# Row sums transposed before their reciprocal, a priority for each step of an attention pair, and a first moment for each weight piece

## The chip, the cores and the metric

The kernel runs on one core of one Trainium2 chip. A time is the device time of one execution in microseconds; "before" is the median of three runs. The core has five queues of instructions that run in order: TensorE (PE, with its weight loads PEld), VectorE (DVE), ScalarE (ACT), GpSimd (POOL) and SyncE (SP), which issues all DMAs here.

## The reference

```python
# 4 batches x 8 heads, 576 positions, head_dim 64
scores = q @ k.T / sqrt(64)
scores = where(block_i >= block_j, scores, -1e9)      # causal by blocks of 64
attn = exp(scores - max(scores))
attn = attn / (sum(attn) + 1e-9)
x = (attn @ v) as 2304 tokens x 512
for w_in, w_out, c in ((moe..., 1.0), (moe2..., 1.702)):
    h = x @ w_in                                      # 512 -> 2048
    x = (h / (1 + exp(-c * h))) @ w_out               # 2048 -> 512
```

The inputs of attention are float32; the weights arrive in float64 and are converted on the chip. Products are made with a high and a low part of each operand (three matmuls in place of one).

## The kernel before

Attention works on 16 pairs (`NP`) of heads; a pair lies on 128 partitions, 64 for each head. For a pair the steps are: load q, k, v; split them into high and low parts (`q_hi`, `q_lo`, `k_hi`, `k_lo`, `v_hi`, `v_lo`) and lay q out as block diagonals (`q_put`, a DMA); for each of nine query blocks j the scores (`s_mm`), their maximum (`s_max`, L423, VectorE) and the exponential (`s_exp`, L433, ScalarE), which also leaves the row sums in column j of the tile `l`; transposes of the exponentials in seven groups (`t_mm`, L472, TensorE), evacuated as a high part (`t_hi`, ScalarE, one of them VectorE) and a remainder (`t_lo`, L490, VectorE); the output products (`o_mm`, L509) and their copies (`o_copy`); three shifts by DMA (`x_shift`), a sum (`x_add`, L537) and a normalization (`x_norm`, L542) on GpSimd.

The row sums go their own way. `r_inv` adds 1e-9 (L439) and takes the reciprocal (L440) of a 128 x 9 tile on VectorE; `r_mm` transposes it into PSUM (L444); `r_copy` copies the 9 x 128 result to SBUF on ScalarE (L450); `r_put` writes it to DRAM (L457) and `r_get` reads it back broadcast (L463), for `x_norm`.

The PSUM banks are handed out in order: scores have fixed banks by j, transposes take turns in banks 4 and 5 (`ring`, `take`), and the transpose of the row sums takes its turn there too, after groups 0, 2 and 6 and before 3, 4, 5 and 1. Output products take turns in banks 6 and 7.

The two feed-forward layers follow: the 16 f-slices of a layer are taken in three passes (`SIZES`), in each pass the tokens in chunks of 512, per chunk and slice 12 matmuls up (L648 to L650), the gate (L663 to L668) and 12 matmuls down (L675 to L677). The weights come in pieces, two for each slice: a DMA of 512 KB into one of two raw buffers (L231), a conversion by ScalarE (L238), four VectorE instructions (L247, L249, L259, L261) and GpSimd (L269), and a split into high and low (L274, L275). Converted pieces of the first slices are made while attention still runs.

The order of all this comes from a planner in the kernel (`Flow`). Each step is added with an engine, an assumed duration, the buffers that it reads and writes, and a priority `at`; `run` then goes through time and lets each engine take, of the steps that are ready at that moment, the one with the lowest `at`. That order becomes the order of instructions in each queue. The chip then runs each queue in that order, whatever the real durations are. Steps of attention always go ahead of those of the feed-forward (`BEFORE`).

Before, the priority of an attention step was its place in the list `plan` (L545): an offset in whole pairs and its index, times `TAU` = 12.6. A weight piece was not ready before `EARLY`: 150 us for piece 0 and 7 us more for each further one, up to piece 8. SBUF pools of attention (`a1`, `a2`, `a3`) are closed and reopened for the feed-forward (`l1`, `l2`, `l3`) when all attention steps listed up to then are done (`ends`, L603).

Of the kernel before, what the change touches and what calls it, by code (L numbers as in the profile page):

```python
# [129 lines left out]
def block_causal_attention_two_ffn(  # L130
# [25 lines left out]
    NS = 10  # L156
    N1, N2 = 2, 3
    NWF = 8
    EARLY = (150.0, 7.0)
    NWARM = 12  # L160
    TAU = 12.6
    LEAD = 8
    BEFORE = 1e4
# [122 lines left out]

    ends = {"a1": [], "a2": [], "a3": []}
    clock = [0.0]

    def op(eng, us, fn, reads=(), writes=(), lag=0.0, size=0, sb=False):  # L290
        x = add(eng, us, fn, reads, writes, clock[0] - BEFORE, lag=lag, size=size, name="att", sb=sb)
        for y in ends:
            ends[y].append(x)
        return x

    def bd(p, i):
# [18 lines left out]
        return T("a3", shape or [P, S], dt, f"{n}_{p % 2}")  # L315

    def pt(p, i):
        return T("a2" if p % 2 == 0 else "a3", [P, nat, P], F32R, f"pt{i}_{p % 2}")

    def copy(eng, o, i):  # L320
        if eng == "act":
# [112 lines left out]
            o, t, AF.Exp, bias=mx_(p, j), scale=1.0, accum_out=ls[:, j:j + 1]),  # L434
            kb + [("mx", p % 2, j)], [kpj(p, j), ("l", p % 2, j)])

    def r_inv(p):
        r, ls = a3(p, "r", [P, NB]), a3(p, "l", [P, NB])
        op("dve", 0.16, lambda: nc.vector.tensor_scalar_add(r, ls, 1e-9), [("l", p % 2, j) for j in range(NB)], [("r", p % 2)])  # L439
        op("dve", 0.2, lambda: nc.vector.reciprocal(out=r, in_=r), [("r", p % 2)], [("r", p % 2)])  # L440

    def r_mm(p):
        b = take("t", ("rp", p))
        op("pe", 0.11, lambda: nc.tensor.transpose(bank[b][:NB, :P], a3(p, "r"), ident), [("r", p % 2), "ident"], [("B", b)],  # L444
           lag=0.2)

    def r_copy(p):
        b = held["rp", p]
        rt = a3(0, "rt", [NB, P])
        op("act", 0.16, lambda: nc.scalar.copy(rt, bank[b][:NB, :P]), [("B", b)], [("rt", 0)])  # L450

    def rd_(p):
        return T("drp", [2, NB, BLK], F32, f"rd{p % 2}")
# [25 lines left out]
    def t_hi(p, g, eng):  # L479
        b = held["t", p, g]  # L480
        n = len(groups[g]) * P
        t = bank[b][:, :n]
        o = pt_view(p, 0, g)
        op(eng, US[eng](n), copy(eng, o, t), [("B", b)], [("pt", p % 2, g, 0)])

    def t_lo(p, g):
        b = held["t", p, g]
        n = len(groups[g]) * P
        hi, lo = (pt_view(p, i, g) for i in range(2))
        op("dve", dve(n), lambda: nc.vector.tensor_sub(lo, bank[b][:, :n], f32(hi)), [("B", b), ("pt", p % 2, g, 0)],  # L490
           [("pt", p % 2, g, 1)])

    def o_mm(p, h, half):
        j0, j1 = halves[half]
        n = (j1 - j0) * BLK
        b = take("o", ("o", p, h, half))
        o = bank[b]
        va = va_(p)
        seq = [(i, kt) for i in (0, 1) for kt in range(NKT) if 2 * kt < j1]
        fs = {fidx[kt, j] for _, kt in seq for j in range(max(j0, 2 * kt), j1)}  # L500
        gs = [g for g, x in enumerate(groups) if fs & set(x)]

        def mms():
            for a, (i, kt) in enumerate(seq):
                js = max(j0, 2 * kt)
                f = fidx[kt, js]
                w = va[:, 2 * kt + h, :, :].rearrange("p a b -> p (a b)")
                x = pt(p, i)[:, f:f + j1 - js, h * BLK:(h + 1) * BLK]
                nc.tensor.matmul(o[:, (js - j0) * BLK:n], w, x, start=(a == 0), stop=(a == len(seq) - 1))  # L509

        us = sum(mm((j1 - max(j0, 2 * kt)) * BLK) * 1.05 for i, kt in seq)
        op("pe", us, mms, [("pt", p % 2, g, i) for g in gs for i in range(2)] + [("va", p % 2, 0), ("va", p % 2, 1)], [("B", b)], lag=0.2)

    def e_(p, h):
        return a3(p, f"e{h}")
# [23 lines left out]
    def x_norm(p):  # L539
# [2 lines left out]
        op("pool", 1.45, lambda: nc.gpsimd.tensor_mul(xy[:, hp, b * S:(b + 1) * S], x, rb),  # L542
           [("x", p % 2, 0), ("x", p % 2, 1), ("rb", p % 2, 0), ("rb", p % 2, 1)], xkeys(hp, b * S, S))

    plan = [  # L545
        (0, s_mm, 3), (1, s_exp, 4), (0, s_max, 3), (2, o_mm, 0, 0), (1, t_mm, 2), (1, t_hi, 0, "act"),
        (3, x_shift, 1), (0, s_exp, 3), (3, x_shift, 2), (0, s_mm, 7), (1, t_hi, 2, "act"),
        (2, o_mm, 0, 1), (-1, q_hi, "act"), (2, o_copy, 0, 0, "dve"), (0, s_mm, 0), (1, r_inv),
        (1, t_lo, 0), (1, t_mm, 6), (0, s_max, 7), (0, s_mm, 8), (1, t_lo, 2), (1, r_mm),
        (0, s_exp, 7), (1, load, "v"), (1, t_hi, 6, "act"), (1, t_lo, 6), (0, s_max, 0), (3, x_add), (-1, load, "k"),  # L550
        (2, o_copy, 0, 1, "act"), (-1, q_lo), (-1, q_put, 0), (0, s_mm, 2), (1, v_hi, "pool"),
        (-1, k_hi, "pool"), (-1, q_put, 1), (0, s_exp, 0), (2, x_shift, 0), (1, t_mm, 3),
        (3, x_norm), (0, s_mm, 6), (2, o_mm, 1, 0), (0, s_max, 2), (1, r_copy),
        (0, s_max, 8), (1, t_hi, 3, "act"), (1, t_mm, 4), (0, s_exp, 2), (0, s_mm, 5), (0, s_max, 6),
        (-1, k_lo, "pool"), (0, s_exp, 8), (-2, load, "q"), (1, t_lo, 3), (2, o_mm, 1, 1),
        (1, t_hi, 4, "act"), (0, s_exp, 6), (0, s_max, 5), (1, t_lo, 4), (2, o_copy, 1, 0, "act"),
        (0, s_exp, 5), (0, s_mm, 1), (1, t_mm, 5), (1, v_lo, "pool"), (1, t_mm, 1), (1, r_put),
        (0, s_max, 1), (0, s_mm, 4), (1, t_hi, 5, "dve"), (2, o_copy, 1, 1, "act"),
        (1, t_lo, 5), (0, s_exp, 1), (1, t_hi, 1, "act"), (2, r_get), (0, s_max, 4), (0, t_mm, 0),
        (1, t_lo, 1),  # L560
    ]

    def attention():
        clock[0] = -1e3
        load(0, "q")
        load(0, "k")
        load(1, "q")
        load(1, "k")
        warm = a1(0, "ql")[:, :512]
        op("dve", 0.5, lambda: nc.vector.memset(f32(warm), 0.0), (), [ka1(0, "ql")])  # L570
        op("pe", 4.7, lambda: [nc.tensor.matmul(bank[7], warm[:, :P], warm, start=True, stop=True) for _ in range(NWARM)],
           [ka1(0, "ql")], [("B", 7)])
        op("pool", 0.6, lambda: make_identity(nc, ident), (), ["ident"])
        op("pool", 0.1, lambda: nc.gpsimd.memset(one, 1.0), (), ["one"])
        for i in range(2):
            for k in range(2):
                t = bd(i, k)
                op("pool", 0.6, lambda t=t: nc.gpsimd.memset(f32(t[A, :, B]), 0.0), (), [("bd", i, k, 0)])
                op("pool", 0.6, lambda t=t: nc.gpsimd.memset(f32(t[B, :, A]), 0.0), (), [("bd", i, k, 1)])
            for j in range(0, NB, 2):  # L580
                op("dve", 0.1, lambda i=i, j=j: nc.vector.memset(pj(i, j)[:, (j + 1) * BLK:], 0.0), (), [kpj(i, j)])
        k_hi(0, "act")
        q, kq = src(0, "q")
        q = q.rearrange("p (j n) -> p j n", n=BLK)
        for h, r in enumerate((A, B)):
            op("act", 0.69, lambda r=r: nc.scalar.mul(bd(0, 0)[r, :, r], q[r], BLK ** -0.5), [kq], [("bd", 0, 0, h)])
        k_lo(0, "pool")
        for h, r in enumerate((A, B)):
            op("dve", 0.9, lambda r=r: q_sub(bd(0, 1)[r, :, r], q[r], bd(0, 0)[r, :, r]), [kq, ("bd", 0, 0, h)],
               [("bd", 0, 1, h)])  # L590
        for p in range(NP + 3):
            for i, (off, fn, *args) in enumerate(plan + [(0, None)]):
                clock[0] = p * TAU + i * TAU / len(plan)
                if fn and 0 <= p - off < NP:
                    fn(p - off, *args)
            if p in (NP - 1, NP, NP + 2):
                k = {NP - 1: 1, NP: 2, NP + 2: 3}[p]

                def swap(k=k):
                    stacks[f"a{k}"].close()  # L600
                    pools[f"l{k}"] = open_pool(ctx, f"l{k}")

                opened[f"l{k}"] = add("none", 0.0, swap, after=list(ends[f"a{k}"]) + [opened[x] for x in opened])  # L603
                ends.pop(f"a{k}")

# [111 lines left out]
    def feed_forward(t):  # L719
        for l in range(2):  # L720
            f0 = 0
            for i, size in enumerate(SIZES[l]):
                fs = list(range(f0, f0 + size))
                f0 += size
                for z, f in enumerate(fs):
                    n = l * NF + f
                    at = -100 + n if n < N1 else t + z * 5.4 - LEAD
                    for h in range(2):
                        o = functools.partial(add, at=at, early=EARLY[0] + EARLY[1] * min(piece(n, h), NWF))
                        w_load(o, n, h)  # L730
                        for stage in (w_scale, w_bits, w_rest, w_sum):
                            stage(o, n, h)
                        w_split(n, h, at)
                t = phase(l, fs, i == 0, i == len(SIZES[l]) - 1, t)
# [50 lines left out]
```

## Time and profile before

| | |
|---|---|
| median of three runs | 1017.42 us (1016.72 to 1021.14) |
| profiled execution | 1021.33 us, its span 1019.5 us |
| mean granted clock of TensorE | 0.993 |
| busy: PE, DVE, ACT, POOL | 988.3, 703.7, 482.5, 326.1 us |
| moved by DMA | 112.67 MB |

A busy share is a mean over stages: attention fills the first 205 us or so, the feed-forward the rest. Line numbers (L439) are those of the kernel before. "Idle before" and "waited for" name what came last before an engine went on; a wait on an engine that isn't the bottleneck costs nothing.

### The profile page before, as it was taken

How to read it: one execution, taken by the hardware profiler on the slowest of the kernel's cores; microseconds unless marked ns; L12 is line 12 of the kernel's file. 1: busy time of each engine (PE TensorE's matmuls, PEld its weight loads, DVE VectorE, ACT ScalarE, POOL GpSimd, SP SyncE). 2: the span in 40 equal slices, each digit the busy share in tenths (PEclk: the TensorE clock that was granted, in tenths of full speed). 3: DMA queues.
4: the chain of work that ended last, by engine and by line, in shares of the span. 5: the costliest groups of instructions: out<-in, count | busy, mean ns of one | idle time of the engine just before them, and what ended most of it. 6: DMA issues, size and time to landing. Idle time of an engine off the chain costs nothing.

```text
span 1019.5 us, 14413 instructions
## 1 busy us (share of the span) xinstructions
PE 988.3 (97%) x5196; PEld 846.5 (83%) x5196; DVE 703.7 (69%) x1144; ACT 482.5 (47%) x1055; POOL 326.1 (32%) x238
## 2 busy tenths in 40 slices
PE   7899998889999999999999999999999999999998
PEld 6888888867888888888888888888898888988887
DVE  6888888999999886749873359863269443444433
ACT  6778778755555452335432245533255222333221
POOL 7566665684444432216320026320035000000000
PEclk9999999989999999999999999999999999999999
DMA  7677779532333344422331111321112222112222
GB/s 188 157 184 184 185 177 219 151 110 92 135 124 138 133 163 166 138 78 86 133 126 61 42 33 61 136 83 42 42 62 83 83 83 83 63 62 83 84 83 83
DMA packets 84616, 112.67 MB, mean 111 GB/s; under 512 B 41920, under 2 KB 46528, under 8 KB 84544
## 3 DMA queue, kind: packets, MB, share of 16 engines
q1 hardware_dynamic: 84544, 111.74, 35.9%
q8 instruction: 41, 0.67, 0.3%
q14 instruction: 31, 0.25, 0.1%
HBM read 72.12 MB, written 23.67 MB: 94 GB/s over the span
## 4 chain that ended last, share of the span: by engine, by line
PE 73%; DVE 15%; ACT 4%; DMA 3%; issue 3%; POOL 1%; SPq 0%; DVEq 0%; ACTq 0%; POOLq 0%
PE bank L648 11%; PE bank L650 11%; PE bank L649 11%; PE sb L675 6%; PE sb L677 6%; PE sb L676 6%; PE bank L677 6%; PE bank L675 6%; PE bank L676 6%; PE bank L509 2%; PE bank L472 2%; DVE wf L249 2%; DVE xc L629 2%; ACT p L433 2%; DVE pt L490 2%
## 5 line engine op out<-in xcount | busy, mean ns | idle before, releaser
L665 DVE SCALAR_TENSOR_TENSOR th<-th,bank 128x512 f32<-128x512 f32 (+1 forms) x160 | 100.4, 629 | 203.6 <-ACT th L663 203.3
L648 PE MATMUL bank<-xc,ws 128*128 128x512 f32 (+1 forms) x640 | 236.6, 370 | 0.0
L649 PE MATMUL bank<-xc,ws 128*128 128x512 f32 (+1 forms) x640 | 236.1, 369 | 0.0
L650 PE MATMUL bank<-xc,ws 128*128 128x512 f32 (+1 forms) x640 | 236.0, 369 | 0.0
L663 ACT ACTIVATE th<-bank 128x512 f32<-128x512 f32 (+1 forms) x160 | 88.9, 556 | 294.1 <-PE bank L650 289.2
L275 POOL TENSOR_TENSOR ws<-wf,ws 128x512 fp32r<-128x512 f32 x64 | 91.7, 1442 | 205.4 <-ACT ws L274 205.4
L269 POOL TENSOR_TENSOR wf<-wf,wt 128x512 f32<-128x512 f32 x64 | 93.9, 1467 | 194.6 <-DVE wt L261 177.5
L667 ACT CAST g<-th 128x512 fp32r<-128x512 f32 (+1 forms) x160 | 92.3, 578 | 115.1 <-DVE th L665 115.0
L668 DVE TENSOR_TENSOR g<-th,g 128x512 fp32r<-128x512 f32 (+1 forms) x160 | 110.9, 695 | 43.4 <-ACT g L667 42.1
L650 PEld LDWEIGHTS bank<-xc,ws 128*128 128x128 f32 x640 | 120.9, 189 | 20.6 <-DVE xc L629 0.5
L648 PEld LDWEIGHTS bank<-xc,ws 128*128 128x128 f32 x640 | 121.2, 189 | 20.3
L649 PEld LDWEIGHTS bank<-xc,ws 128*128 128x128 f32 x640 | 121.1, 189 | 20.0
L677 PE MATMUL sb<-g,ws 128*128 128x512 f32 (+1 forms) x320 | 118.4, 370 | 2.4 <-DVE g L668 2.3
L675 PE MATMUL sb<-g,ws 128*128 128x512 f32 (+1 forms) x320 | 118.5, 370 | 1.6 <-DVE yst L710 0.5
L676 PE MATMUL sb<-g,ws 128*128 128x512 f32 (+1 forms) x320 | 117.8, 368 | 0.0
L675 PE MATMUL bank<-g,ws 128*128 128x512 f32 (+1 forms) x320 | 117.7, 368 | 0.0
L676 PE MATMUL bank<-g,ws 128*128 128x512 f32 (+1 forms) x320 | 117.7, 368 | 0.0
L677 PE MATMUL bank<-g,ws 128*128 128x512 f32 (+1 forms) x320 | 117.7, 368 | 0.0
L629 DVE TENSOR_TENSOR xc<-xy,xc 128x512 fp32r<-128x512 f32 (+1 forms) x120 | 90.9, 777 | 14.0 <-PE bank L649 8.5
L490 DVE TENSOR_TENSOR pt<-bank,pt 128x512 fp32r<-128x512 f32 (+1 forms) x112 | 68.7, 620 | 15.2 <-ACT pt L322 15.1
L627 ACT CAST xc<-xy 128x512 fp32r<-128x512 f32 (+1 forms) x120 | 66.8, 575 | 25.1 <-PE bank L649 23.7
L472 PE MATMUL bank<-ident,p 128*128 128x128 f32 x400 | 63.9, 284 | 11.1 <-DVE pt L490 9.7
(76 smaller groups left out, 1623.7 us busy)
## 6 DMA issues: line engine op xcount, KB each, us to landing
raw<-w SPq DMA_DIRECT2D x64, 512.0 KB, 3.5
yd<-yst SPq DMA_DIRECT2D x64, 256.0 KB, 2.4
yst<-yd SPq DMA_DIRECT2D x64, 256.0 KB, 4.1
v<-vP SPq DMA_DIRECT2D x16, 320.0 KB
k<-kT SPq DMA_DIRECT2D x16, 288.0 KB, 3.8
rb<-rd SPq DMA_DIRECT2D x32, 144.0 KB, 3.7
x<-e SPq DMA_DIRECT2D x32, 144.0 KB, 3.1
q<-qT SPq DMA_DIRECT2D x15, 288.0 KB, 3.6
```

Source lines behind the costliest of these rows:

```text
L269: op("pool", 1.27, lambda: nc.gpsimd.tensor_add(wf_(k), wf_(k), wt_(k)), [kw, kt], [kw])
L275: add("pool", 1.28, lambda: nc.gpsimd.tensor_sub(slot(n, i)[:, 1, :], wf_(k), f32(slot(n, i)[:, 0, :])), [kw, kh], [kl], at, after=slot_af ...
L629: add("dve", dve(n) + 0.01, lambda view=view, s=s: nc.vector.tensor_sub(view(1), s, f32(view(0))), xkeys(kt, c0, n) + [Kh], [Kl], tx, afte ...
L648: nc.tensor.matmul(h, w[:, 0, c], view(0), start=kt == 0, stop=False)
L649: nc.tensor.matmul(h, w[:, 1, c], view(0), start=False, stop=False)
L650: nc.tensor.matmul(h, w[:, 0, c], view(1), start=False, stop=kt == ND - 1)
L665: add("dve", dve(n), lambda th=th, h=h: nc.vector.scalar_tensor_tensor(out=th(), in0=th(), scalar=1.0, in1=h, op0=ALU.add, op1=ALU.mult), ...
L667: add("act", act(n) + 0.05, lambda th=th, g=g: nc.scalar.copy(g(0), th()), [kth], [kgh], t, after=e2)
L668: add("dve", dve(n) + 0.01, lambda th=th, g=g: nc.vector.tensor_sub(g(1), th(), f32(g(0))), [kth, kgh], [kgl], t, after=e2, sb=True)
L675: nc.tensor.matmul(y, w[:, 0, c], g(0), start=st, stop=False)
L676: nc.tensor.matmul(y, w[:, 1, c], g(0), start=False, stop=False)
L677: nc.tensor.matmul(y, w[:, 0, c], g(1), start=False, stop=sp)
```

## The change

The row sums `l` are transposed as they are (`r_mm` reads `l`); `r_inv` then runs on the 9 x 128 block: VectorE adds 1e-9 from PSUM into `rt` and takes the reciprocal in place. `r_copy` is gone. Each step of a pair gets a number of its own, in pair lengths from the pair's start, and the pairs are listed one after the other; each weight piece gets its own first moment; a pool is closed when the steps that read or write its own tiles are done. `NPT` = 2 leaves `pt` as it was. The explicit early load of k for pair 1 is left to the plan.

```diff
-    EARLY = (150.0, 7.0)
+    EARLY = [146.9, 164.9, 159.8, 120.4, 105.5, 214.8, 0.0, 153.2, 224.6, 111.5, 211.0, 126.0]
+    NPT = 2
...
-        for y in ends:
-            ends[y].append(x)
+        for k in [*reads, *writes]:
+            home = {"q": "a1", "k": "a1", "qh": "a1", "ql": "a1", "kh": "a1", "kl": "a1", "bd": "a1", "pj": "a2"}.get(k[0], "a3")
+            if k[0] == "pt" and NPT == 2 and k[1] == 0:
+                home = "a2"
+            ends[home].append(x)
...
-    def r_inv(p):
-        r, ls = a3(p, "r", [P, NB]), a3(p, "l", [P, NB])
-        op("dve", 0.16, lambda: nc.vector.tensor_scalar_add(r, ls, 1e-9), [("l", p % 2, j) for j in range(NB)], [("r", p % 2)])
-        op("dve", 0.2, lambda: nc.vector.reciprocal(out=r, in_=r), [("r", p % 2)], [("r", p % 2)])
-
     def r_mm(p):
         b = take("t", ("rp", p))
-        op("pe", 0.11, lambda: nc.tensor.transpose(bank[b][:NB, :P], a3(p, "r"), ident), [("r", p % 2), "ident"], [("B", b)],
-           lag=0.2)
-
-    def r_copy(p):
+        op("pe", 0.11, lambda: nc.tensor.transpose(bank[b][:NB, :P], a3(p, "l"), ident),
+           [("l", p % 2, j) for j in range(NB)] + ["ident"], [("B", b)], lag=0.2)
+
+    def r_inv(p):
         b = held["rp", p]
         rt = a3(0, "rt", [NB, P])
-        op("act", 0.16, lambda: nc.scalar.copy(rt, bank[b][:NB, :P]), [("B", b)], [("rt", 0)])
+        op("dve", 0.2, lambda: nc.vector.tensor_scalar_add(rt, bank[b][:NB, :P], 1e-9), [("B", b)], [("rt", 0)])
+        op("dve", 0.2, lambda: nc.vector.reciprocal(out=rt, in_=rt), [("rt", 0)], [("rt", 0)])
...
     plan = [
-        (0, s_mm, 3), (1, s_exp, 4), (0, s_max, 3), (2, o_mm, 0, 0), (1, t_mm, 2), (1, t_hi, 0, "act"),
...
+        (-2.723, load, "q"), (1.183, q_hi, "act"), (-1.280, load, "k"), (-0.183, q_lo), (-0.345, q_put, 0),
...
+        (4.531, s_exp, 3), (-0.564, s_mm, 7), (2.002, s_mm, 0), (-0.949, s_max, 7), (-0.149, s_mm, 8),
...
+        (1.031, s_exp, 8), (0.947, s_exp, 6), (0.482, s_max, 5), (-4.074, s_exp, 5), (3.642, s_mm, 1),
+        (-3.963, s_max, 1), (-1.298, s_mm, 4), (1.450, s_exp, 1), (-0.863, s_max, 4), (-2.689, t_mm, 0),
+        (1.367, s_exp, 4), (-3.165, t_mm, 2), (3.487, t_hi, 0, "act"), (4.445, t_hi, 2, "act"), (1.334, t_lo, 0),
+        (2.779, t_mm, 6), (-0.926, t_lo, 2), (1.165, r_mm), (5.767, load, "v"), (4.163, t_hi, 6, "act"),
+        (-1.842, t_lo, 6), (2.135, v_hi, "pool"), (1.312, t_mm, 3), (2.570, r_inv), (0.963, t_hi, 3, "act"),
+        (1.268, t_mm, 4), (1.074, t_lo, 3), (0.524, t_hi, 4, "act"), (3.748, t_lo, 4), (1.079, t_mm, 5),
...
+        (-0.868, t_hi, 1, "act"), (0.639, t_lo, 1), (3.600, o_mm, 0, 0), (1.750, o_mm, 0, 1),
+        (-0.616, o_copy, 0, 0, "dve"), (-0.169, o_copy, 0, 1, "act"), (3.637, x_shift, 0), (6.914, o_mm, 1, 0),
+        (5.482, o_mm, 1, 1), (-0.296, o_copy, 1, 0, "act"), (1.063, o_copy, 1, 1, "act"), (4.455, r_get),
+        (3.644, x_shift, 1), (0.122, x_shift, 2), (2.699, x_add), (7.925, x_norm),
     ]
...
+        for p in range(NP):
+            for i, (when, fn, *args) in enumerate(plan):
...
+                        clock[0], tag[0] = (p + when) * TAU, f"{p}.{i}"
+                        fn(p, *args)
+        for k in (1, 2, 3):
...
+            opened[f"l{k}"] = add("none", 0.0, swap, after=ends[f"a{k}"] + [opened[x] for x in opened])
...
-                        o = functools.partial(add, at=at, early=EARLY[0] + EARLY[1] * min(piece(n, h), NWF))
+                        o = functools.partial(add, at=at, early=EARLY[min(piece(n, h), len(EARLY) - 1)], name=f"c.{piece(n, h)}")
```

## Rows read from the trace of the kernel before

**Rows 1.** Busy time by stretch: from:to, length, engines (instructions), clock, DMA share, GB/s
```profile
30.00:204.00 174.00, 159.44 (x1157) 148.20 (x1156) 150.15 (x302) 135.44 (x402) 112.98 (x81) 0.98 0.73 182
204.00:217.00 13.00, 10.49 (x66) 9.22 (x65) 11.86 (x19) 8.80 (x20) 12.42 (x8) 0.82 0.49 140
217.00:231.00 14.00, 12.31 (x52) 9.14 (x51) 13.12 (x14) 7.66 (x14) 9.89 (x7) 0.92 0.25 71
231.00:255.00 24.00, 23.54 (x102) 18.55 (x101) 23.84 (x32) 12.76 (x22) 9.21 (x7) 1.00 0.27 99
255.00:1000.00 745.00, 743.08 (x3582) 627.14 (x3581) 475.90 (x717) 293.58 (x533) 161.63 (x112) 1.00 0.27 92
```

**Rows 2.** What PE waited for, 30 to 204 us: us in total, times, longest
```profile
PE bank L472 <- DVE pt L490: 6.1, 11, 1.6
PE bank L410 <- ACT p L433: 2.6, 5, 0.8
PE bank L444 <- DVE r L440: 2.1, 2, 1.3
PE sb L410 <- ACT p L433: 1.9, 3, 1.1
PE bank L509 <- DVE e L325: 1.1, 1, 1.1
PE bank L444 <- DVE pt L490: 0.2, 1, 0.2
```

**Rows 3.** The chain of waits, 30 to 204 us, its shares by line
```profile
by line: PE bank L472 9.9%; PE bank L509 9.3%; DVE pt L490 7.7%; ACT p L433 7.2%; DVE mx L423 6.3%; DMA q<-qT 4.5%; DMA bd<-qh 4.4%; DMA k<-kT 4.3%; DVE ql L358 4.0%; DVE r L439 3.8%; ACT pt L322 3.4%; issue 3.3%; PE bank L410 3.1%; PE bank
```

**Rows 4.** What PE waited for, 204 to 255 us; then two moments of its timeline
```profile
PE bank L472 <- DVE pt L490: 2.8, 3, 1.4
PE sb L677 <- DVE g L668: 1.7, 2, 1.3
PE sb L675 <- ACT g L667: 0.4, 1, 0.4
...
203.16 0.28 PE L412 MATMUL bank<-kh,bd 128*128 128x128 f32 x1
203.70 0.66 PE L472 MATMUL bank<-ident,p 128*128 128x128 f32 x4 [0.26 <-DVE pt L490]
```

**Rows 5.** Groups by shape, 30 to 204 us: count | busy us, mean ns | idle before
```profile
L439 DVE TENSOR_SCALAR r<-l 128x9 f32<-128x9 f32 x14 | 14.1, 1006 | 0.0
...
L325 DVE CAST pt<-bank 128x128 fp32r<-128x128 f32 x14 | 3.9, 279 | 0.0
...
L450 ACT COPY rt<-bank 9x128 f32<-9x128 f32 x14 | 3.5, 253 | 7.6 <-PE bank L444 6.4 <-DMA bd<-qh 1.0
L440 DVE RECIPROCAL r<-r 128x9 f32<-128x9 f32 x14 | 2.9, 204 | 0.1
```

**Rows 6.** The add's line: shortest, median and longest in ns, first and last start
```profile
L439 DVE TENSOR_SCALAR r<-l x16: 164/887/1404, 16.7 to 204.4; 128x9 f32<-128x9 f32 x16
```

**Rows 7.** Timeline, VectorE beside GpSimd, at 54 and at 192 us
```profile
54.23 1.95 POOL L377 TENSOR_TENSOR kl<-k,kh 128x576 fp32r<-128x576 f32 x1
54.81 1.40 DVE L439 TENSOR_SCALAR r<-l 128x9 f32<-128x9 f32 x1
...
192.07 1.44 POOL L542 TENSOR_TENSOR xy<-x,rb 128x576 f32<-128x576 f32 x1
192.19 0.20 DVE L440 RECIPROCAL r<-r 128x9 f32<-128x9 f32 x1
```

**Rows 8.** What GpSimd waited for, 30 to 204 us (one line of it)
```profile
POOL va L324 <- DMA v<-vP: 8.0, 3, 4.3
```

**Rows 9.** Timeline of SP: the first weight load, the second, and the sixth
```profile
158.24 0.41 SPq L231 DMA_DIRECT2D raw<-w  x1
169.33 0.42 SPq L231 DMA_DIRECT2D raw<-w  x1
...
212.55 0.44 SPq L231 DMA_DIRECT2D raw<-w  x1
```

More of the change, by code (lines that the diff above doesn't have):

```diff
@@ L288, in block_causal_attention_two_ffn @@
     clock = [0.0]
+    tag = ["att"]
     def op(eng, us, fn, reads=(), writes=(), lag=0.0, size=0, sb=False):
-        x = add(eng, us, fn, reads, writes, clock[0] - BEFORE, lag=lag, size=size, name="att", sb=sb)
-        for y in ends:
-            ends[y].append(x)
+        x = add(eng, us, fn, reads, writes, clock[0] - BEFORE, lag=lag, size=size, name=tag[0], sb=sb)
+        for k in [*reads, *writes]:
[3 more added lines that the diff above has]
+            ends[home].append(x)
         return x
@@ L317, in pt @@
     def pt(p, i):
-        return T("a2" if p % 2 == 0 else "a3", [P, nat, P], F32R, f"pt{i}_{p % 2}")
+        return T("a2" if p % NPT == 0 and NPT == 2 else "a3", [P, nat, P], F32R, f"pt{i}_{p % NPT}")
     def copy(eng, o, i):
@@ L483, in t_hi @@
         o = pt_view(p, 0, g)
-        op(eng, US[eng](n), copy(eng, o, t), [("B", b)], [("pt", p % 2, g, 0)])
+        op(eng, US[eng](n), copy(eng, o, t), [("B", b)], [("pt", p % NPT, g, 0)])
     def t_lo(p, g):
@@ L489, in t_lo @@
         hi, lo = (pt_view(p, i, g) for i in range(2))
-        op("dve", dve(n), lambda: nc.vector.tensor_sub(lo, bank[b][:, :n], f32(hi)), [("B", b), ("pt", p % 2, g, 0)],
-           [("pt", p % 2, g, 1)])
+        op("dve", dve(n), lambda: nc.vector.tensor_sub(lo, bank[b][:, :n], f32(hi)), [("B", b), ("pt", p % NPT, g, 0)],
+           [("pt", p % NPT, g, 1)])
     def o_mm(p, h, half):
@@ L511, in o_mm @@
         us = sum(mm((j1 - max(j0, 2 * kt)) * BLK) * 1.05 for i, kt in seq)
-        op("pe", us, mms, [("pt", p % 2, g, i) for g in gs for i in range(2)] + [("va", p % 2, 0), ("va", p % 2, 1)], [("B", b)], lag=0.2)
+        op("pe", us, mms, [("pt", p % NPT, g, i) for g in gs for i in range(2)] + [("va", p % 2, 0), ("va", p % 2, 1)], [("B", b)], lag=0.2)
     def e_(p, h):
@@ L545, in block_causal_attention_two_ffn @@
     plan = [
-        (0, s_mm, 3), (1, s_exp, 4), (0, s_max, 3), (2, o_mm, 0, 0), (1, t_mm, 2), (1, t_hi, 0, "act"),
[L547 to L560, printed above, removed]
+        (-2.723, load, "q"), (1.183, q_hi, "act"), (-1.280, load, "k"), (-0.183, q_lo), (-0.345, q_put, 0),
+        (-2.686, k_hi, "pool"), (0.980, q_put, 1), (0.245, k_lo, "pool"), (-1.194, s_mm, 3), (0.748, s_max, 3),
@@ new lines, in block_causal_attention_two_ffn @@
+        (4.531, s_exp, 3), (-0.564, s_mm, 7), (2.002, s_mm, 0), (-0.949, s_max, 7), (-0.149, s_mm, 8),
+        (-2.167, s_exp, 7), (1.002, s_max, 0), (1.724, s_mm, 2), (-0.588, s_exp, 0), (2.067, s_mm, 6),
+        (-0.682, s_max, 2), (1.749, s_max, 8), (-1.264, s_exp, 2), (-0.360, s_mm, 5), (1.084, s_max, 6),
+        (1.031, s_exp, 8), (0.947, s_exp, 6), (0.482, s_max, 5), (-4.074, s_exp, 5), (3.642, s_mm, 1),
+        (-3.963, s_max, 1), (-1.298, s_mm, 4), (1.450, s_exp, 1), (-0.863, s_max, 4), (-2.689, t_mm, 0),
@@ new lines, in block_causal_attention_two_ffn @@
+        (1.367, s_exp, 4), (-3.165, t_mm, 2), (3.487, t_hi, 0, "act"), (4.445, t_hi, 2, "act"), (1.334, t_lo, 0),
+        (2.779, t_mm, 6), (-0.926, t_lo, 2), (1.165, r_mm), (5.767, load, "v"), (4.163, t_hi, 6, "act"),
+        (-1.842, t_lo, 6), (2.135, v_hi, "pool"), (1.312, t_mm, 3), (2.570, r_inv), (0.963, t_hi, 3, "act"),
+        (1.268, t_mm, 4), (1.074, t_lo, 3), (0.524, t_hi, 4, "act"), (3.748, t_lo, 4), (1.079, t_mm, 5),
+        (-0.675, v_lo, "pool"), (3.757, t_mm, 1), (0.319, r_put), (-1.531, t_hi, 5, "dve"), (2.700, t_lo, 5),
@@ L567, in attention @@
         load(1, "q")
-        load(1, "k")
         warm = a1(0, "ql")[:, :512]
@@ L590, in attention, with swap @@
                [("bd", 0, 1, h)])
[L591 to L604, printed above, removed]
+        for p in range(NP):
+            for i, (when, fn, *args) in enumerate(plan):
+                if p > 0 or fn not in (load, q_hi, q_lo, q_put, k_hi, k_lo) or args == ["v"]:
+                    if (p, fn, args) != (1, load, ["q"]):
+                        clock[0], tag[0] = (p + when) * TAU, f"{p}.{i}"
+                        fn(p, *args)
+        for k in (1, 2, 3):
+            def swap(k=k):
+                stacks[f"a{k}"].close()
+                pools[f"l{k}"] = open_pool(ctx, f"l{k}")
+            opened[f"l{k}"] = add("none", 0.0, swap, after=ends[f"a{k}"] + [opened[x] for x in opened])
     nstep = [0]
```

## The prediction

> **What bounds the kernel now.** I read five views in this order: busy time by stretch, who waited for whom on TensorE, the chain of waits, the groups of instructions by shape, and the issues of the weight loads.
>
> By stretch [rows 1]: after 255 us TensorE is busy 743.1 of 745 us at full clock. That part is bound by its own matmuls, the change doesn't touch their number, and it can only be shifted as a whole. What can change is how soon it begins, so the change is worth what it takes from the first 255 us. In the steady attention (30 to 204 us, 14 pairs, 12.4 us each) no engine is full: TensorE 159.4 of 174 us, VectorE 150.2, ScalarE 135.4, GpSimd 113.0. The pairs are held by a round of waits among nearly full engines. TensorE's idle time there is 174 - 159.4 = 14.6 us, and the waits name 14.0 of it [rows 2]: 6.1 us for the remainders of the transposed blocks (L490), 4.5 us for exps that free a score bank (2.6 + 1.9), 2.1 us for the reciprocal (L440), 1.1 us for an output copy, 0.2 us at L444 for L490. The chain of waits puts 3.8% of 174 us, 6.6 us, on the add of 1e-9 (L439) alone [rows 3]. From 204 to 255 us TensorE waits 4.9 us by name [rows 4], and its clock falls to 0.82 and 0.92 of full in the two stretches with gaps [rows 1].
>
> **The row sums.** Out per pair, by the means of 30 to 204 us [rows 5]: the add, 1.006 us; the reciprocal, 0.204 us; the ScalarE copy, 0.253 us. The add is nine columns and has taken 0.164 us at its shortest, 1.404 at its longest [rows 6]; the long ones end with a GpSimd instruction, as at 54.81 us, where it ends at 56.21 and GpSimd's L377 at 56.18 [rows 7]. So most of the 1.006 us is waiting. The reciprocal doesn't wait so: at 192.19 us it took 0.20 with a GpSimd instruction under way [rows 7].
>
> In per pair: an add that reads PSUM, 9 x 128. A PSUM to SBUF cast of 128 columns took 0.279 us in all 14 pairs [rows 5]; I take that. And a reciprocal of 128 columns instead of nine, which no row shows. Low end: one column costs no more than in the cast, and it takes the cast's 0.28. High end: the whole 0.204 us of nine columns goes by the column, 128/9 x 0.204 = 2.9. In between: what the nine columns took beyond the shortest add, 0.204 - 0.164 = 0.040 us, goes by the column on top of a 128-column instruction, 0.28 + 128/9 x 0.040 = 0.85. I take 0.85, since it uses the one row of the same operation and charges only its excess. VectorE per pair: 0.28 + 0.85 - 1.006 - 0.204 = -0.08 us, times 16 is -1.3 us; the ends are 16 x -0.65 = -10.4 and 16 x +1.97 = +31.5. VectorE is busy 86% of the stretch, so about -1 us reaches the end. ScalarE gives up 16 x 0.253 = 4 us, worth nothing by itself: it has 38 us of idle time there.
>
> The Trainium skill ("VectorE: DVE Perf Modes", section "First, the fixed hardware budget") says that Reciprocal runs as an iterative divide with a repeat count of 8. Read as eight cycles a column at the page's 0.96 GHz, that estimates 128 columns at 1.07 us and the fixed part at 0.28, 1.35 in all, and speaks against this change; no run here shows it yet, and rows 5 and 6 alone give 0.85. By the page the term of -1 us would be about +7.
>
> In order: the transpose (r_mm) now waits for the last exp instead of for the reciprocal. Before it in its bank ring come t_mm 0, 2 and 6, and t_mm 2 already reads the block of the last exp, so the 2.1 us wait on L440 goes with nothing late in its place: -2 us (bounds 0 to -2.1). What is late next is the bank: it was freed by a ScalarE copy, and is now freed by an add in VectorE's queue. Behind it on TensorE stands t_mm 4, the next user of that bank, and every matmul after it. If the add comes first in VectorE's queue, nothing; if one 0.68 us remainder stands ahead, that much per pair (rival 3). The DMA of the result (r_put) waits for the reciprocal, then r_get and x_norm: a chain with GpSimd at 65% and nothing urgent behind it until the last pair.
>
> **The priorities.** The steps keep their number, instructions and DMAs; only which ready one an engine takes first changes, and the planner writes that into each queue. On TensorE, t_mm 0 and 2 move forward by 3.7 and 4.2 pair lengths and the output products of head 1 back by 2.8 and 4.4; on VectorE, s_max 1 forward by 4.8; on ScalarE, s_exp 5 forward by 4.9, t_hi 0 and 2 and s_exp 3 back by 2.4 to 4.4. On SP the loads of q and k move forward by 1.4 and 0.6, that of v back by 4.5, past the q_put, r_put, x_shift and r_get of its own pair and of later ones; GpSimd waited 8.0 us for v before and bore it [rows 8], with 61 us idle. Most of these figures never decide anything, because few steps are ready at once. No row prices an order that hasn't run. The bounds: all of the remaining named TensorE waits go (6.1 + 4.5 + 1.1 = 11.7 us), or the same amount comes on top. I take a gain of somewhat under half, 5 us: the forward moves (transposes and scores first, output products as filler) are at the two kinds of wait that carry 10.6 of the 11.7 us. Each engine's idle time is the cover; VectorE's 23.9 us is the thinnest and can't give much more than that.
>
> **The weight pieces and the pools.** The weight instructions stay the same; the planned first moments move: piece 0 by -3 us, 1 by +8, 2 by -4, 5 by +30, 8 by +19. The real issues came later than planned (the first at 158.2 for 150, the sixth at 212.6 for 185) because each waits for one of two raw buffers [rows 9], so the moments are mostly a matter of order. The pools that close early now wait only for their own readers; the last score product ends at about 203.4 us and the first pool's last listed step at about the same time [rows 4], so that is worth about 0. I put the whole start of the feed-forward at 0, between -4.9 (all waits of 204 to 255 us) and +5.
>
> **The sum.** -2 (wait on the reciprocal), -1 (VectorE), -5 (order), 0 (start of the feed-forward) = -8 us. The profiled execution took 1021.33 us, 1019.5 of it the span, so it would become 1013.3; against the median of the three runs, 1017.42, it is 1009.4, and that is my number.
>
> **The rivals.**
> 1. The reciprocal of 128 columns costs only 0.28. For it: neighbouring VectorE rows go by the column alone. Against it: the 0.040 us excess. VectorE then gives 10.4 us, 86% of it 9 instead of 1: 1001.4.
> 2. The gain is given back at the start of the feed-forward: attention ends earlier, but pieces 5 and 7 are held to 214.8 us and later, and TensorE waits for them. For it: VectorE is full from 217 to 255 (37.0 of 38 us). Against: TensorE waited there for no weight [rows 4]. 8 less about 6: 1015.
> 3. Slower: the bank of the row sums stays held behind VectorE's queue. It decides from the point where one 0.68 us remainder or more stands ahead of the add and t_mm 4 is next on TensorE; the order gains nothing, and 16 x 0.68 = 11 us is lost: 1028. For it: r_inv's priority is 2.57, behind most s_max of the next pair. Against: the planner sees this dependence.
> 4. The reciprocal goes by the column more than I took, a good way from 0.85 towards its bound of 2.9. For it: the nine columns' excess may hide part of what a column costs. Against: nothing but that row. At 1.5 us VectorE's queue grows by 0.28 + 1.5 - 1.21 = 0.57 us a pair, 16 x 0.57 = +9 us instead of -1: 1019. The Trainium skill ("VectorE: DVE Perf Modes", "First, the fixed hardware budget") has a rule that leads there, the divide with its repeat count of 8; by the estimate above it would give 1017.
>
> **Chances.** Forecast 0.40 (0.03 of it for one that falls short); rival 1 0.15; rival 2 0.14; rival 3 0.18; rival 4 0.13 (0.02 of it over +0.5%). Half a per cent, 5.1 us, is about what a measurement of this kernel can tell from no change. Faster: 0.37 + 0.15 = 0.52; same: 0.14 + 0.11 + 0.03 = 0.28; slower: 0.18 + 0.02 = 0.20. The range reaches from a fast reciprocal with a good order, 997, to most of rival 3, 1026; the forecast's own range is 1005 to 1012.
>
> **What would show it.** Right: no wait of L444's successor on the reciprocal; the new add near 0.28 us and never over 0.7; the reciprocal near 0.85; the last score product at about 196 instead of 203; TensorE full from about 224. Wrong: TensorE waiting for the new add (rival 3); ScalarE or GpSimd weight splits as releasers of the first feed-forward matmuls (rival 2); a reciprocal near 0.3 (rival 1) or over 1 us (rival 4); or a pair length still at 12.4 us.

## The result, and the profile after

| | before | after |
|---|---|---|
| median (four runs each) | 1017.53 us | 1009.75 us |
| profiled execution, its span | 1021.33, 1019.5 us | 1010.5, 1008.7 us |

Ratio 0.9915, 95% interval 0.9889 to 0.9941: by the ratio 8.6 us faster, 6.0 to 11.3 (the medians differ by 7.8). The profiled execution of the kernel before is the longest of its four, so the two traces differ by more, 10.8 us of span. The sum of -8 us was close. Its terms were not, as the experiments show.

Line numbers move by one to five: in the changed kernel L444 is still the transpose of the row sums, L450 the add from PSUM, L451 the reciprocal, L473 the transposes, L491 their remainders, L510 the output products, L415 to L417 the scores, L232 the weight loads.

Busy time by stretch, changed kernel, same columns as [rows 1]:

```profile
30.00:204.00 174.00, 165.53 (x1213) 156.20 (x1211) 157.18 (x316) 143.81 (x406) 121.12 (x86) 0.97 0.76 187
204.00:217.00 13.00, 10.62 (x43) 8.22 (x42) 12.85 (x13) 3.26 (x7) 10.03 (x7) 0.82 0.25 67
217.00:231.00 14.00, 14.00 (x62) 11.58 (x63) 9.77 (x12) 5.68 (x11) 6.58 (x5) 1.00 0.24 86
231.00:255.00 24.00, 24.00 (x108) 19.87 (x107) 23.35 (x34) 15.33 (x29) 8.29 (x6) 1.00 0.19 66
```

What TensorE waited for from 30 to 204 us, answering to [rows 2]: the wait for the reciprocal is gone, the others fell from 11.9 us to 7.9, and only 0.8 of that lies before 165 us.

```profile
PE bank L473 <- DVE pt L491: 3.9, 5, 1.9
PE sb L415 <- ACT p L438: 1.7, 1, 1.7
PE bank L510 <- DVE e L330: 1.7, 1, 1.7
PE sb L415 <- issue: 0.6, 1, 0.6
```

The chain of waits over the same stretch, answering to [rows 3]: it now runs through TensorE's own lines (L510, L473, L415 to L417), where before it was spread over TensorE, VectorE, ScalarE and DMAs.

```profile
by line: PE bank L510 26.5%; PE bank L473 20.8%; PE bank L417 6.6%; PE bank L415 6.5%; PE bank L416 6.4%; PE sb L415 5.8%; PE sb L416 3.6%; PE sb L417 3.6%; issue 3.5%; DVE pt L491 3.3%; DVE mx L428 2.9%; DVE wf L250 2.4%; DVE wt L248 1.8%;
```

The new add and the reciprocal, by line (shortest, median, longest in ns), answering to [rows 5, 6]: the times of either vary by 5 ns at most, so neither waits as the old add did.

```profile
L450 DVE TENSOR_SCALAR rt<-bank x16: 267/268/272, 19.4 to 196.7; 9x128 f32<-9x128 f32 x16
L451 DVE RECIPROCAL rt<-rt x16: 929/930/932, 20.8 to 198.3; 9x128 f32<-9x128 f32 x16
```

How long a pair takes is read from the spacing of an instruction that comes once a pair. Two successive transposes of the row sums, first in the kernel before, then in the changed one:

```profile
118.54 0.27 PE L444 MATMUL bank<-ident,r 128*9 128x128 f32 x1
130.04 0.28 PE L444 MATMUL bank<-ident,r 128*9 128x128 f32 x1 [0.77 <-DVE r L440]
```

```profile
109.41 0.27 PE L444 MATMUL bank<-ident,l 128*9 128x128 f32 x1
120.50 0.27 PE L444 MATMUL bank<-ident,l 128*9 128x128 f32 x1
```

Over eleven pairs, from reciprocal to reciprocal, it was 12.17 us before (31.03 to 164.90) and 11.12 after (32.67 to 154.98). The before value is a mean over unequal pairs, the after value one repeated to 0.1 us. The last pairs of the changed kernel are longer: its last four transposes of row sums are 12.0, 14.6 and 15.3 us apart. Here are the last score product and the last transpose of row sums of the changed kernel:

```profile
188.49 0.28 PE L417 MATMUL bank<-kh,bd 128*128 128x128 f32 x1
...
195.84 0.27 PE L444 MATMUL bank<-ident,l 128*9 128x128 f32 x1
```

The first is 14.7 us earlier than before (203.16, [rows 4]), the second 10.1 earlier (205.92 before). The last output product of attention (L509, now L510) starts at 210.09 us in place of 220.74, 10.65 earlier; it tells best how much sooner attention is done, since the new order moves scores ahead of other steps. The last three pairs share VectorE with the weight pieces, and the granted clock is 0.82 in 204 to 217 us, as it was before. The first six weight loads, answering to [rows 9]; between the fifth and the sixth, whose planned first moment is 214.8, there is a hole of 18 us:

```profile
145.95 0.34 SPq L232 DMA_DIRECT2D raw<-w  x1
166.10 0.59 SPq L232 DMA_DIRECT2D raw<-w  x1
169.60 0.41 SPq L232 DMA_DIRECT2D raw<-w  x1
184.86 0.33 SPq L232 DMA_DIRECT2D raw<-w  x1
196.82 0.34 SPq L232 DMA_DIRECT2D raw<-w  x1
214.98 0.82 SPq L232 DMA_DIRECT2D raw<-w  x2
```

### The profile page after: what moved, and what is told of

Read it like the earlier page. It is cut to its first block, busy times and chain, and to the rows that moved or that the text cites. A ratio compares the mean times of both kernels' runs of the same rounds, so it can differ in the third digit from the quotient of the medians.

```text
span 1008.7 us, 14443 instructions
## 1 busy us (share of the span) xinstructions
PE 985.2 (98%) x5196; PEld 847.3 (84%) x5196; DVE 697.2 (69%) x1144; ACT 481.9 (48%) x1039; POOL 325.9 (32%) x238
## 4 chain that ended last, share of the span: by engine, by line
PE 83%; DVE 11%; issue 3%; ACT 2%; POOL 1%; DMA 1%; DVEq 0%; SPq 0%; ACTq 0%; POOLq 0%
PE bank L649 11%; PE bank L650 11%; PE bank L651 11%; PE sb L676 6%; PE sb L678 6%; PE sb L677 6%; PE bank L676 6%; PE bank L677 6%; PE bank L678 6%; PE bank L510 5%; PE bank L473 4%; DVE xc L630 2%; DVE wf L250 2%; DVE g L669 2%; PE bank L415 1%
## 5 line engine op out<-in xcount | busy, mean ns | idle before, releaser
L669 DVE TENSOR_TENSOR g<-th,g 128x512 fp32r<-128x512 f32 (+1 forms) x160 | 114.9, 720 | 44.6 <-ACT g L668 43.5
L630 DVE TENSOR_TENSOR xc<-xy,xc 128x512 fp32r<-128x512 f32 (+1 forms) x120 | 95.2, 815 | 15.2 <-PE bank L650 9.7
L491 DVE TENSOR_TENSOR pt<-bank,pt 128x512 fp32r<-128x512 f32 (+1 forms) x112 | 69.5, 624 | 9.6 <-ACT pt L327 9.5
L676 PEld LDWEIGHTS sb<-g,ws 128*128 128x128 f32 x320 | 60.3, 189 | 16.2 <-DVE yst L706 2.9
```

What stands on the lines that cost most here:

```text
L630: add("dve", dve(n) + 0.01, lambda view=view, s=s: nc.vector.tensor_sub(view(1), s, f32(view(0))), xkeys(kt, c0, n) + [Kh], [Kl], tx, afte ...
L669: add("dve", dve(n) + 0.01, lambda th=th, g=g: nc.vector.tensor_sub(g(1), th(), f32(g(0))), [kth, kgh], [kgl], t, after=e2, sb=True)
L676: nc.tensor.matmul(y, w[:, 0, c], g(0), start=st, stop=False)
```

## The experiments

Pair lengths below are means over eleven pairs, from reciprocal to reciprocal as above (in the kernel without a reciprocal from transpose to transpose). Each ratio is to the kernel before on the same chip.

**The parts, one at a time.** First the row sums alone, in the old list:

```diff
 # kernel before
-    r_inv (add, reciprocal on l), r_mm, r_copy
+    r_mm (transposes l), r_inv (add from PSUM, reciprocal)
-    plan: (1, r_inv) ... (1, r_copy)
+    plan: (1, r_inv) in the place of r_copy
```

> The kernel before with the new path of the row sums alone (transposed first, add and reciprocal on the 9 x 128 block, no ScalarE copy; they stand at the old copy's place in the list). Theory: the path trades VectorE time about evenly (0.27 + 0.93 in, 1.006 + 0.204 out) and only the wait on the reciprocal goes, so 1014 to 1018, a quarter of the gain at most. Rival (the row sums are the whole gain): 1009 to 1011. Rival (bank held behind VectorE's queue): over 1020.

1016.71 us, ratio 0.9982 (0.9971 to 0.9992); a pair 12.14 us, or 11.95 from transpose to transpose, where the kernel before has 12.28. The path alone gives 1.8 us (0.8 to 3.0), in a list that the planner wrote anew around it.

```diff
 # changed kernel
-        (1.165, r_mm), ... (2.570, r_inv)
+        (1.165, r_inv), (1.165, r_mm), ... (2.570, r_copy)      # with the old functions
```

> The changed kernel with the old path of the row sums (add and reciprocal on 128 x 9, transpose, ScalarE copy) under the new priorities and first moments. Theory: most of the gain is the order, so 1009 to 1013, and a pair stays near 11.1 us. Rival (the add's wait for GpSimd is what the change removes): 1015 or more, the add again at 1 us in the mean and a pair over 12 us.

1027.42 us, ratio 1.0084 (1.0070 to 1.0099); a pair 12.55 us. That is slower than before, and my theory fell: with the new priorities and first moments the old path loses. Part of the 8.6 us can be the first moments (6.4 us by themselves, below); the longer pair is not theirs, since they leave it at 12.13 us. TensorE waits for the reciprocal again. What it waited for from 30 to 204 us, and the add's line:

```profile
PE bank L477 <- DVE pt L495: 6.1, 13, 0.9
PE bank L449 <- DVE r L445: 4.9, 3, 1.7
...
L444 DVE TENSOR_SCALAR r<-l x16: 164/934/1437, 17.1 to 212.7; 128x9 f32<-128x9 f32 x16
```

These are the rival's signs (the add took 0.85 us in the mean). But the run can't say whether the add's wait or the list is to blame, since three steps in place of two make the planner write another list. The next two kernels change the first moments alone.

```diff
 # changed kernel
-    EARLY = [146.9, 164.9, 159.8, ...]
+    EARLY = [150.0 + 7.0 * i for i in range(9)]
```

> The changed kernel with the old first moments (150 us and 7 us more for each piece). Theory: 1008 to 1013; the loss of the last pairs, where a pair takes 12 to 17 us instead of 11.1, is there with either list. Rival (the moments carry the gain): 1015 or more.

1005.99 us, ratio 0.9878 (0.9861 to 0.9895); a pair 11.11 us. The new first moments seem to cost the change something: its own ratio is 0.9915, 3.8 us more, with intervals that overlap at their edges (0.9889 and 0.9895). In the traces the last output product starts at 206.50 us in place of 210.09, and the spans are 1003.4 and 1008.7. The same moments in the kernel before:

```diff
 # kernel before
-    EARLY = (150.0, 7.0)
+    EARLY = [146.9, 164.9, 159.8, ...]
```

> The kernel before with the new first moments of the weight pieces alone. Theory (the moments matter little): 1015 to 1020. Rival (they are half of the gain): 1013 or less.

1024.43 us, ratio 1.0063 (1.0047 to 1.0080): 6.4 us slower, outside of both expectations. The pair length (12.13 us) is that of before. The trace can't place the whole loss: its span is only 1.3 us longer than that of the kernel before (1020.8 and 1019.5), whose traced execution was a long one. It does show a difference where the feed-forward begins. What TensorE waited for there, 204 to 255 us, against [rows 4]:

```profile
PE bank L650 <- DVE xc L629: 3.4, 2, 2.4
PE bank L648 <- ACT xc L627: 2.3, 1, 2.3
PE bank L472 <- DVE pt L490: 1.5, 1, 1.5
PE sb L677 <- DVE g L668: 0.2, 1, 0.2
```

It waits 5.7 us for the split inputs of a chunk (`xc`), for which it waited nothing before. That these waits are the 6.4 us is not shown.

```diff
 # kernel before
-        for y in ends: ends[y].append(x)
+        each step only into the list of the pools whose tiles it reads or writes
```

> The kernel before with the new rule for closing the SBUF pools alone (a pool waits for its own readers only). Theory: the last readers end where the last listed steps end, 1016 to 1020. Rival (an earlier start of the feed-forward): 1014 or less.

1019.12 us, ratio 1.0009 (0.9997 to 1.0020). As expected: nothing.

**The add's wait, with the list held fixed.** Two kernels change one instruction and leave every queue in its order.

```diff
 # kernel before; the add of 1e-9 is left out
-    tensor_scalar_add(r, ls, 1e-9); reciprocal(out=r, in_=r)
+    reciprocal(out=r, in_=ls)
```

> The kernel before, every queue in the same order, but the add of 1e-9 is left out and the reciprocal reads the row sums directly. Theory (the add's wait for GpSimd sits in the round of waits that sets the pair's length): the 1.0 us a pair goes and most of it reaches the end, a pair falls from 12.4 to about 11.7 us, 1007 to 1012. Rival (the wait is covered, or the next VectorE instruction inherits it): 1015 to 1018.

1013.70 us, ratio 0.9945 (0.9932 to 0.9958), 5.6 us faster; a pair 11.66 us. The time lands between the two expectations; the gain is at the low end of the theory's, since the kernel before took 1019.49 us on this chip. Of 16 x 1.0 us, about a third reaches the end. TensorE from 30 to 204 us no longer waits for the reciprocal, and less for the remainders (4.2 instead of 6.1 us), which stand behind the add in the list:

```profile
PE bank L472 <- DVE pt L490: 4.2, 8, 1.4
PE bank L410 <- ACT p L433: 2.6, 5, 0.8
PE sb L410 <- ACT p L433: 1.8, 3, 1.0
PE bank L509 <- DVE e L325: 1.1, 1, 1.1
```

```diff
 # changed kernel
+    tensor_scalar_add(r, ls, 1e-9)                       # the old add, result unused
     tensor_scalar_add(rt, bank[b][:NB, :P], 1e-9)
```

> The changed kernel, every queue in the same order, with one VectorE instruction more for each pair: the old add of 1e-9 on 128 x 9 in SBUF, ahead of the new add, its result unused. Theory: it waits for GpSimd again and a pair grows from 11.1 by 0.3 to 0.9 us: 1014 to 1022. Rival (in the new order VectorE has room, 9.8 of 11 us busy): 1009 to 1012.

1012.07 us, ratio 0.9930 (0.9918 to 0.9941), against 0.9915: 1.5 us, and the intervals overlap, so the rival was nearer. A pair grows only to 11.38 us. The old add does wait again, but less at its new place (its median was 887 ns, [rows 6]):

```profile
L451 DVE TENSOR_SCALAR r<-l x16: 164/349/1256, 19.4 to 198.1; 128x9 f32<-128x9 f32 x16
L451 DVE TENSOR_SCALAR rt<-bank x16: 270/271/279, 19.8 to 199.2; 9x128 f32<-9x128 f32 x16
```

**What bounds the new pair.** The reciprocal is left out, every queue in its order:

```diff
 # changed kernel
-    reciprocal(out=rt, in_=rt)
```

> The changed kernel, every queue in the same order, with the reciprocal left out (the output is then scaled wrongly by design of the test). It prices the 0.93 us reciprocal. Theory: TensorE is full in the steady pairs, so only the pairs that share VectorE with the weights gain: 1006 to 1009. Rival (VectorE sets the pair's length): 1000 or less.

1007.13 us, ratio 0.9881 (0.9868 to 0.9894): 3.4 us less than the change, with intervals that overlap at their edges. A pair stays at 11.13 us, so 0.93 us less on VectorE is worth nothing in the steady pairs, and the gain lies in the last ones (the last two transposes of row sums are 12.7 us apart in place of 15.3). VectorE isn't the bound in the steady pairs.

```diff
 # changed kernel with the old first moments; the add of 1e-9 is left out
-    tensor_scalar_add(rt, bank[b], 1e-9); reciprocal(out=rt, in_=rt)
+    reciprocal(out=rt, in_=bank[b])
```

> A version meant to beat both: the changed kernel with the old first moments (1006.0 by its own run) and without the add of 1e-9, the reciprocal reading PSUM directly; every queue in the order of that run. A row sum holds exp(0) = 1 at least, so 1e-9 is below half a unit of the last place in float32. Theory: 0.27 us less a pair on VectorE, worth 0 in the steady pairs and a little in the last ones: 1003 to 1006. Rival (a reciprocal that reads PSUM holds the bank for 0.93 us instead of 0.27, and t_mm 4 waits): 1007 or more.

1012.31 us, ratio 0.9938 (0.9925 to 0.9952): 6 us slower than the same kernel with the add, as the rival said; a pair is 11.60 us in place of 11.11. The reciprocal takes 935 ns when it reads PSUM and holds the transposes' bank all that time. But it also took the add's place in VectorE's queue, so it now runs ahead of the maximum of a 192-column score block, behind which it ran before. The changed kernel, then this one:

```profile
110.21 0.34 DVE L428 TENSOR_REDUCE mx<-bank 128x1 f32<-128x192 f32 x1
110.48 0.93 DVE L451 RECIPROCAL rt<-rt 9x128 f32<-9x128 f32 x1
```

```profile
113.32 0.93 DVE L450 RECIPROCAL rt<-bank 9x128 f32<-9x128 f32 x1
114.19 0.87 DVE L428 TENSOR_REDUCE mx<-bank 128x1 f32<-128x192 f32 x2
```

At the time I saw the bank alone, and thought that the two banks of the transposes set 11.1 us. The next kernel gives the row sums columns of their own:

```diff
 # changed kernel
-    r_mm writes, r_inv reads   bank[b][:NB, :P]
+    r_mm writes, r_inv reads   sb[:NB, 1, 384:512]       # unused columns of bank 3
```

> The changed kernel, every queue in the same order, with the transposed row sums in unused columns of bank 3 in place of a turn in banks 4 and 5. Theory (the two banks of the transposes set the pair's length, since holding one 0.66 us longer took a pair from 11.1 to 11.6 us): a pair falls to 10.7 to 11.0 us and the time to 1003 to 1007. Rival (TensorE's own work sets 11.1 us): a pair stays at 11.1 us, 1009 to 1011.

1011.26 us, ratio 0.9931 (0.9914 to 0.9948); a pair 11.33 us, longer. The theory fell, and the rival's 11.1 us didn't come either, because the edit brings a wait of its own. The row sums now lie in the tile `sb` of a score block, and what reads that block waits for them: VectorE's maximum for L444, where it waited for the score product, and ScalarE's exp for the add, where it waited for the maximum. From 30 to 165 us, first in the changed kernel, then in this one:

```profile
DVE mx L428 <- PE sb L417: 4.5, 12, 0.4
ACT p L438 <- DVE mx L428: 8.3, 24, 1.7
```

```profile
DVE mx L428 <- PE sb L444: 5.8, 12, 0.5
ACT p L438 <- DVE rt L450: 7.5, 11, 0.7
ACT p L438 <- DVE mx L428: 4.2, 13, 1.7
```

What a pair then loses is seen on TensorE by the step from one start to the next. The lines below are four transposes (`t_mm` 4) and the 384-column score product behind them, which needs the bank that the exp of the 192-column block frees. First the changed kernel, then this one, then the one whose reciprocal reads PSUM:

```profile
110.95 0.60 PE L473 MATMUL bank<-ident,p 128*128 128x128 f32 x4
111.30 0.42 PE L415 MATMUL bank<-kh,bd 128*128 128x384 f32 x1
```

```profile
112.44 0.60 PE L473 MATMUL bank<-ident,p 128*128 128x128 f32 x4
112.99 0.45 PE L415 MATMUL bank<-kh,bd 128*128 128x384 f32 x1
```

```profile
114.31 0.66 PE L473 MATMUL bank<-ident,p 128*128 128x128 f32 x4
115.07 0.45 PE L415 MATMUL bank<-kh,bd 128*128 128x384 f32 x1
```

The step is 0.35, 0.55 and 0.76 us. In the last kernel the transposes also start late, and 0.11 us in all is lost at them for the bank that the reciprocal holds; about 0.35 is lost at the score product, for the late maximum. In the pair at 110 us every other step between matmuls is the same to 0.02 us in the three kernels. So the 0.49 us of the kernel before this one was mostly the maximum's turn, and the bank was the lesser part.

The busy share doesn't show such gaps: from 30 to 150 us TensorE counts as busy for 120.00 of 120 us in the changed kernel and for 119.98 in this one, since a matmul's recorded time reaches over them. What speaks for TensorE's own work as the bound of the steady pair is that its steps, and its 11.11 to 11.13 us, are the same in the changed kernel, without the reciprocal and with either other set of first moments.

With the old first moments the same edit gave:

> A version meant to beat both: the changed kernel with the old first moments and the row sums in unused columns of bank 3. Theory: 1006.0 less what the bank gives, 1000 to 1004. Rival: 1005 to 1007.

1009.14 us, ratio 0.9910 (0.9893 to 0.9926), 3 us worse than without it (1005.99); a pair is 11.33 us here too.

**The weight pieces.** Later still:

```diff
 # changed kernel
+    EARLY = [165.0 + 7.0 * i for i in range(9)]
```

> The changed kernel with first moments of 165 us and 7 us more for each piece, 15 us later than the old ones. Theory (weight pieces and pairs compete for VectorE in the last three pairs; what a later start gives the pairs, the feed-forward loses for want of pieces): 1005 to 1010, no better than the 1006.0 of 150 us. Rival (the later the better): 1002 or less. Rival (the pieces are needed at once): over 1012.

1007.68 us, ratio 0.9891 (0.9875 to 0.9907): as the theory had it, no better than 150 us. TensorE counts as full from 30 to 165 us (135.00 of 135, and 133.29 with the moments of 150 us) and then has less in 204 to 217 us. Later moments, then the old ones, then those of the change, each from 204 to 217 us:

```profile
204.00:217.00 13.00, 9.57 (x42) 6.87 (x42) 12.93 (x14) 6.08 (x11) 9.13 (x7) 1.00 0.36 106
```

```profile
204.00:217.00 13.00, 12.04 (x56) 9.56 (x56) 12.83 (x15) 6.05 (x11) 8.56 (x6) 1.00 0.42 122
```

The row of the change stands above (10.62 of 13, at a clock of 0.82). VectorE is full in all three. The best version run is the changed kernel with the old first moments, 1005.99 us: faster than the kernel before by 12.4 us and than the change by about 4.

## Why the prediction was right, and where only its sum was

**The wait on the reciprocal, -2 us.** Right in kind: no wait at L444 is left, and the forecast that t_mm 2 already waits for the last exp held.

**VectorE's time for the row sums, -1 us.** The durations were nearly right: 0.268 for the add (0.28 forecast) and 0.930 for the reciprocal (0.85), 1.198 in against 1.210 out. As a term it was mis-sized, because I traded the add's waiting against the reciprocal's working one for one. They aren't worth the same: the add with its wait was worth 5.6 us in the old list, while the reciprocal costs about 3.4 us in the new one and nothing in a steady pair. The path alone, in the old list, gave 1.8 us (0.8 to 3.0) where my two terms said 3.

Eight cycles a column, as the prediction read the repeat count of 8 in the Trainium skill ("VectorE: DVE Perf Modes", "First, the fixed hardware budget"), gave an estimate of 1.35 us and +7 us; the trace disagrees, at 0.930. From 9 to 128 columns it grew from 0.204 to 0.930, 6.1 ns a column, which is between one cycle and eight at the 0.96 GHz of the Trainium skill ("VectorE: DVE Perf Modes", "Specifications"). Rival 1 (0.28 us) and rival 4 (1.5 us) fell both, by the same row.

That the old add waits and the new one doesn't has a rule in the Trainium skill ("SBUF — State Buffer", "Who interferes with whom"): a tensor_scalar can enter a mode with two ports, in which it and GpSimd block each other for a whole instruction; outside such a mode, an instruction with at most one SBUF input doesn't contend. The trace agrees: 14 of the 16 old adds end 26 to 36 ns after a GpSimd instruction and take up to 1404 ns, the other two take 164 and 173; the new add, whose input is in PSUM, takes 267 to 272.

**The order, -5 us.** Right in direction, and half the size. With the old first moments the change is 12.4 us faster; less the 1.8 of the path that leaves 10.6. I had taken somewhat under half of the named TensorE waits. In fact the steady pairs came down to TensorE's own 11.1 us. [rows 1] nearly had that number, 159.44 us busy over 14 pairs, 11.4 each; with the 12.17 us that a pair really took (my 12.4 was 174 us over 14), the bound is 14 x (12.17 - 11.12) = 15 us. But the 10.6 is what is left over, no run has the order alone, and path and order can't be priced apart: order and new moments with the old path are 8.6 us slower than before. One reason that fits, though no run separates it: the planner assumed 0.16 us for the old add, which measured 1.006.

**The start of the feed-forward, 0 us.** This term failed: "the moments are mostly a matter of order" was so, but order there isn't free. The new moments cost 6.4 us alone and about 3.8 with the new order, inside my +5 with the change and outside it alone. With the new order, 3.6 of the 5.3 us between the two traces are lost before the last output product, in the last pairs, and not at the start of the feed-forward. Rival 2, that the feed-forward gives the gain back, did not happen: the last output product came 10.65 us sooner than in the kernel before and the span became 10.8 us shorter. That the last score product came 14.7 us sooner was in part only its new place in the order. Attention's output products reach to 220.7 us in the kernel before, not to about 205. Nor did TensorE wait for the splits of held pieces. From 165 to 255 us it waits mostly for what VectorE is late with (3.1 us for remainders, 1.7 for a copy, 1.1 for the gate, against 3.0 for ScalarE). The pools were worth nothing, as forecast.

**Rival 3** didn't occur: TensorE waited for the new add nowhere in the changed kernel. Nor is its mechanism shown at that price: where the reciprocal held the same bank 0.66 us longer, the transposes lost 0.11 us of a pair's 0.49, and most of the rest came from a maximum that stood behind it. Its 1028 also leaves out my -3 for path and wait; with it the price is 1025.

So: -1.8, -10.6 and +3.8 make -8.6, where I had -3, -5 and 0. This split makes the sum by its construction, since the -10.6 is a remainder, but two of its numbers are measured and neither is mine. The sum was close because errors cancelled, and that was luck.

What stays open: what the order is worth with the old path and the old moments, and how much of the cost of the new moments is the clock. Up to 255 us, the profiled run with the old ones has a lower clock in 190 to 204 us only (0.79) beside 0.98 in 165 to 190, the change in all of 165 to 217 (0.93, 0.80, 0.82). TensorE had been less than full in the stretch where it fell, in both kernels. No run separated the clock from the moments.

## What to carry to other kernels

An order written by a planner rests on the durations that it assumes: look first for the instruction whose shortest and longest time differ by a factor of eight, and take away what it waits for. Then check what the steady part is bound by, by its spacing and by leaving one instruction out, and compare the steps between starts rather than the busy share, which counted two kernels as full whose pairs differ by 0.2 us. Once the spacing equals the busiest engine's own work, what remains to be won lies in the ends. When you leave out one instruction, look at what takes its place in the queue. And test every part of a change alone and with the rest, even if the sum came out right: here one part was a loss.

## What the runs showed of the hardware

A reciprocal on VectorE took 0.204 us for 128 x 9, 0.930 for 9 x 128 from SBUF and 0.935 from PSUM: about 6 ns for each further column. The 1152 elements are the same; nine of 128 partitions make it 4.6 times as long. An add of nine columns between SBUF operands (0.164 us) took up to 1.4 us beside GpSimd; the reciprocal of the same shape never took over 0.219, though a GpSimd instruction was under way throughout 10 of its 16. A write to unused columns of a tile in this program moved the waits of its readers: ScalarE's exps waited 7.5 us in all for the add that reads those columns, though they read none of them, and a pair took 0.2 us more.
